# A planner's due times shifted by a table: attention and two expert layers on one core

## The chip, the cores and the metric

The kernel runs on one core of a Trainium2 chip. The metric is the device time of one execution in microseconds, as the median of several runs. A profiled execution has a time of its own and a span, which runs from its first instruction to its last.

## What is computed

Three steps follow each other on 2304 tokens (4 batches of 576). Everything comes in and goes out in float32.

1. Attention with 8 heads of width 64. Heads 0 to 3 see a causal window of 32 keys; heads 4 to 7 see the causal keys whose position agrees with the query's modulo 32. Softmax, then the product with v.
2. `h = x @ w_in` (512 to 2048), then the rational function `g = P(h) / (Q(h) + 1e-6)` with `P = a0 + a1 h + a2 h² + a3 h³` and `Q = 1 + |b0||h| + |b1|h²`, then `g @ w_out` (2048 to 512).
3. `h = x @ w_in` (512 to 1024), softmax of h times h, a layer norm over the 1024 columns, then `@ w_out` (1024 to 512).

## The kernel before

**Number format.** The large products run in float16 with a high and a low part, three matmuls for one. A weight matrix comes in as 64-bit words. `w_load` brings one group of it with one DMA, `w_conv` puts each word's bits together with three VectorE instructions (one `tensor_scalar`, two `scalar_tensor_tensor`) and sums the squares on ScalarE, `w_scales` takes a power of two from that, and `w_split` writes the high part on ScalarE and the low part on VectorE. `w_in` and `w_out` of the first layer have eight groups each ("wi" 0 to 7 and "wo" 0 to 7). All eight wi groups are wanted by the first complete pass of `mm_h`, all eight wo groups by the first `mm_y`.

**Work.** A batch of attention is 12 units: `attn_scores2` or `attn_scores1` (TensorE), `attn_softmax` (row maxima, VectorE), `attn_exp` (ScalarE), `attn_norm` (POOL), `attn_tp`, `attn_tpe`, `attn_pv` (TensorE, ScalarE, TensorE), and `attn_xhi`, `attn_xlo`, which write the block of tokens `xs`. The first layer has nine blocks of 256 tokens with eight groups each. One group is `mm_h` (24 matmuls), about ten elementwise instructions on ScalarE, VectorE and POOL (`a_abs`, `v_q1`, `p_qm`, `v_p2`, `v_p3`, `a_ln`, `a_ex`, `v_t`, `v_rn`, `v_g`, `a_hi`, `p_lo`), and five groups later `mm_y` (24 matmuls). `g_scale` works out the coefficients `ih` and `ac` that `a_abs` needs: 17 tiny POOL instructions and a few of VectorE, once for each batch; it needs the largest |v| of the batch (`v_max`, two long VectorE reductions) and of the weights (`w_pmax`). The second layer takes tiles of 128 tokens (`mm_in2`, the `m_` functions, two transposing DMAs, `mm_out2`, `out_evac`).

**Order.** Nothing is issued while these functions run. `Order.record` collects every call as an operation, numbered in the order of the source: 7549 in all. `Order.run` works out which operation must wait for which (`pre`, `then`), then a due time for each (`first_due`), and four times in turn plans the whole kernel forward (`forward`) and, from the end found, sets new due times (`backward`). The plan that ends first in the planner's own reckoning is kept and `emit` issues its instructions in that order; line 413 is the call that issues them all, which is why every row of the profile bears L413. `forward` goes by time: on each engine it takes, of the operations that could begin within 0.05 us of the earliest, the one with the smallest `due`. Costs of operations, lags between engines, DMA landings, the port that VectorE and POOL share and a rule for TensorE's clock are built into `cost`, `lag` and `forward`. Each engine then carries out its own list strictly in that order, each instruction waiting for what it depends on; the DMAs stand in one list, SP's.

**Which operation has which number** (for the entries of the table that the prediction speaks of): 4 and 5 load q and k of heads 0 and 1, 7 loads the window heads' values `vl`, 11 is wi 0, 14 loads `vs`, 15 is wi 1, 18 and 19 load further q and k, 21 and 27 to 31 are wi 2 to 7, and 32 to 48 build masks and the identity. 49 to 57 are `v_max(0)` and `x_scale(0)`. 58 to 458 are the 12 units of batch 0 with the four pairs of wi groups between them. 459 to 481 are `w_pmax` and the first `g_scale`. 482 to 485 load wo 0 to 3, 486 to 493 load q, k and v of batch 1, and 499 to 556 convert wo 0 to 3 around `mm_h(0, 0)`. 567 to 586 are `g_scale(2)`, for batch 1: 17 POOL instructions and three of VectorE. 637 to 651 and 713 to 732 convert wo 4 to 7. From 733 on the steps of the main loop follow each other, up to 7548.

Of the kernel before, what the change touches and what calls it, by code (L numbers as in the profile page):

```python
# [111 lines left out]
class Order:  # L112
# [136 lines left out]
    def run(self):  # L249
        ops = self.ops  # L250
        for i, op in enumerate(ops):
            op.then = list(op.post)
            for v in op.values:
                v.__dict__.setdefault("users", []).append(i)
        for q in self.queues.values():
            for v, w in zip(q, q[len(q[0].homes):]):
                for j in v.users:
                    if j < w.users[0]:
                        ops[j].then.append(w.users[0])
        for op in ops:  # L260
            op.before = []
        for i, op in enumerate(ops):
            for j in op.then:
                ops[j].before.append(i)
        self.first_due()
        best = None
        for k in range(self.TURNS):
            seq, end, homes = self.forward()
            if best is None or end < best[0]:
                best = (end, seq, homes)  # L270
            if k < self.TURNS - 1:
                self.backward(end)
        _, seq, homes = best
        for v, h in homes:
            v.home = h
        return seq

    TURNS = 4
    WINDOW, ENOUGH = 3.4133, 2800.0
# [1137 lines left out]
```

## Time and profile before

| | us |
|---|---|
| median of 3 runs | 756.23 (755.44 to 756.89) |
| the profiled execution's own time | 757.08 |
| its span | 755.3 |
| TensorE matmul busy | 699.9 (93% of the span) |
| VectorE busy | 547.1 (72%) |
| ScalarE busy | 489.8 (65%) |
| POOL busy | 353.0 (47%) |

The mean granted TensorE clock of the span is 0.948 of 2.4 GHz. In the page's forty slices of the span TensorE is busy for nine tenths or more in every one from the eighth to the thirty-ninth, and of the first seven only in the second; the granted clock is 0.5 to 0.7 in the second to sixth slice and at 0.9 or more in all others.

A row of windows gives, for one stretch, its length, then busy time and count of instructions for PE (TensorE matmul), PEld (its weight loads), DVE (VectorE), ACT (ScalarE) and POOL, then the granted TensorE clock as a share of 2.4 GHz, the mean busy share of the 16 DMA engines and GB/s. A row of the timeline gives start, length, engine, line, operation, what it writes <- what it reads, shapes, count, and in brackets the idle time before it with what ended it. A row of waits gives who waited, for whom, the total, how often, and the longest. In grouped rows the numbers behind the bar are busy us and mean ns of one.

### The profile page before, as it was taken

What the parts mean: (1) busy time and instruction counts of PE and PEld (TensorE: products, weight loads), DVE (VectorE), ACT (ScalarE), POOL (GpSimd) and SP (SyncE); (2) the same over time, 40 slices, a digit from 0 to 9 for tenths busy, and PEclk for the clock granted to TensorE, in tenths of its full rate; (3) what the DMA queues carried; (4) which work ended last, traced back from release to release, by engine and by line L of the source; (5) the groups of instructions that cost most, each with busy time, mean ns of one, the idle gap of its engine ahead of it and who ended that gap; (6) DMA issues with size and microseconds to landing.
All of it is one profiled execution on the core that took longest, in us unless ns stands there. A gap on an engine that the chain in (4) does not pass through costs nothing.

```text
span 755.3 us, 14378 instructions
## 1 busy us (share of the span) xinstructions
PE 699.9 (93%) x5406; PEld 531.7 (70%) x5406; DVE 547.1 (72%) x1114; ACT 489.8 (65%) x1155; POOL 353.0 (47%) x380
## 2 busy tenths in 40 slices
PE   3975368999999999999999999999999999999997
PEld 3763256898888888787777777777776776765443
DVE  6789899689968997787775577576565766644571
ACT  2787558869789679977766676465655646533451
POOL 3233659755689667776434343533534334320000
PEclk9575569999999999999999999999999999999999
DMA  9996801133421321303202010110201011011244
GB/s 270 312 273 167 223 1 34 35 131 127 132 65 60 117 72 34 83 16 62 62 15 43 1 43 1 44 33 10 43 1 43 21 23 43 1 43 43 56 78 103
DMA packets 68101, 55.98 MB, mean 74 GB/s; under 512 B 39616, under 2 KB 56000, under 8 KB 67520
## 3 DMA queue, kind: packets, MB, share of 16 engines
q1 hardware_dynamic: 68032, 55.07, 28.1%
q8 instruction: 42, 0.69, 0.4%
q14 instruction: 27, 0.22, 0.1%
HBM read 40.90 MB, written 4.72 MB: 60 GB/s over the span
## 4 chain that ended last, share of the span: by engine, by line
PE 84%; DVE 7%; ACT 3%; POOL 2%; issue 2%; DMA 1%; SPq 0%; ACTq 0%; DVEq 0%
PE bank L413 46%; PE banks L413 38%; POOL tiny L413 2%; DMA qkb<-in_qk_dram 1%; DVE tiny L413 1%; DVE wi_l L413 1%; DVE T L413 1%; DVE gtb L413 1%; DVE wo_l L413 1%; ACT e L413 1%; DVE p L413 1%; ACT p L413 1%; ACT wo_h L413 0%; DVE bank L413 0%; ACT ysb L413 0%
## 5 line engine op out<-in xcount | busy, mean ns | idle before, releaser
L413 PE MATMUL bank<-xs,wi_h 128*128 128x256 f16 x1152 | 200.0, 278 | 4.0 <-DVE xs L413 2.5
L413 PE MATMUL bank<-xs,wi_l 128*128 128x256 f16 x576 | 159.9, 278 | 1.3 <-DVE wi_l L413 1.3
L413 PE MATMUL banks<-gtb,wo_h 128*128 128x256 f16 x896 | 151.4, 273 | 0.9 <-ACT ysb L413 0.9
L413 PEld LDWEIGHTS <-wi_h 128*128 128x128 f16 x1248 | 124.2, 100 | 30.7 <-issue 4.1
L413 PEld LDWEIGHTS <-wo_h 128*128 128x128 f16 x1152 | 111.7, 98 | 22.1 <-issue 0.9
L413 POOL TENSOR_SCALAR q<-A,aba 128x512 f32<-128x512 f32 x72 | 66.2, 919 | 129.4 <-ACT A L413 129.2
L413 PE MATMUL banks<-gtb,wo_l 128*128 128x256 f16 x448 | 122.1, 273 | 1.7 <-ACT ysb L413 1.7
L413 DVE SCALAR_TENSOR_TENSOR p<-p,ac,bank 128x512 f32<-128x512 f32 x144 | 106.5, 744 | 3.1 <-ACT A L413 0.7
L413 POOL TENSOR_TENSOR gtb<-p,gtb 128x512 f16<-128x512 f32 x56 | 66.8, 1194 | 75.2 <-ACT gtb L413 75.2
L413 DVE TENSOR_TENSOR p<-p,bank 128x512 f32<-128x512 f32 x72 | 49.2, 684 | 69.2 <-ACT p L413 68.7
L413 POOL TENSOR_TENSOR q<-q,A 128x512 f32<-128x512 f32 x72 | 91.7, 1273 | 4.3
L413 PE MATMUL banks<-wi_h,ysb 128*128 128x512 f16 x288 | 90.7, 379 | 0.0
L413 ACT ACTIVATE A<-bank,ih 128x512 f32<-128x512 f32 x72 | 49.6, 689 | 50.8 <-PE bank L413 48.0
L413 DVE SCALAR_TENSOR_TENSOR q<-q,bank 128x512 f32<-128x512 f32 x72 | 49.3, 685 | 34.7 <-ACT bank L413 25.3
L413 PEld LDWEIGHTS <-ysb 128*128 128x128 f16 x432 | 42.1, 98 | 43.8
L413 PE MATMUL bank<-wo_h,T 128*128 128x512 f16 x224 | 70.6, 379 | 0.0
L413 PEld LDWEIGHTS <-wi_l 128*128 128x128 f16 x576 | 57.3, 99 | 12.3 <-issue 3.1
L413 ACT ACTIVATE gtb<-p 128x512 f16<-128x512 f32 x56 | 35.3, 630 | 41.0 <-DVE p L413 41.0
L413 PEld LDWEIGHTS <-wo_l 128*128 128x128 f16 x576 | 56.4, 98 | 7.6 <-issue 0.8
L413 ACT ACTIVATE L<-q 128x512 f32<-128x512 f32 x72 | 45.3, 630 | 24.3 <-POOL q L413 24.0
L413 ACT ACTIVATE p<-bank,ac 128x512 f32<-128x512 f32 x72 | 56.0, 777 | 3.0 <-PE bank L413 3.0
L413 PEld LDWEIGHTS <-T 128*128 128x128 f16 x336 | 32.9, 98 | 34.6
(257 smaller groups left out, 1429.0 us busy)
## 6 DMA issues: line engine op xcount, KB each, us to landing
qkb<-in_qk_dram SPq DMA_DIRECT2D x28, 304.0 KB, 4.6
out_dram<-ot SPq DMA_DIRECT2D x18, 256.0 KB, 2.4
wo_h<-in_w_out_dram SPq DMA_DIRECT2D x4, 1024.0 KB, 5.4
wo_l<-in_w_out_dram SPq DMA_DIRECT2D x4, 1024.0 KB, 7.8
vl<-in_v_dram SPq DMA_DIRECT2D x4, 768.0 KB, 5.1
wi_h<-in_w_in_dram SPq DMA_DIRECT2D x3, 1024.0 KB, 5.4
wi_l<-in_w_in_dram SPq DMA_DIRECT2D x3, 1024.0 KB, 4.9
wo_h<-in_w_in_dram SPq DMA_DIRECT2D x3, 1024.0 KB, 17.3
```

What stands on the lines that cost most here:

```text
L413: getattr(self.real[op.eng], op.call)(*[real(x) for x in op.a], **{k: real(x) for k, x in op.k.items()})
```

## The change

After the four turns the due times of the best turn are put back, each entry of a table `MOVES` is added to them, and the kernel is planned forward once more with the result. An entry is (seed, first, last, by): with seed 0 every operation from `first` up to but not including `last` gets `by` added; with another seed each of them gets `by` times its own number from a normal distribution drawn with that seed. There are 143 entries, 90 with seed 0 and 53 with another, and 61 of them begin below number 1500. No operation is added or left out and none gets other operands, but a buffer's place within its ring follows the order in which the plan asks for it.

```diff
+            due = [op.due for op in ops]
             seq, end, homes = self.forward()
             if best is None or end < best[0]:
-                best = (end, seq, homes)
+                best = (end, seq, homes, due)
             if k < self.TURNS - 1:
                 self.backward(end)
-        _, seq, homes = best
+        _, seq, homes, due = best
+        if self.MOVES:
+            for i, op in enumerate(ops):
+                op.due = due[i]
+            self.moved(self.MOVES)
+            seq, _, homes = self.forward()
...
+    MOVES = (
+        (927833, 2501, 2901, 0.2), (0, 3124, 3128, 2), (335053, 301, 361, 0.2), (764359, 2520, 2580, 2),
+        (473896, 27, 1527, 0.2), (93203, 88, 148, 1), (0, 485, 505, -4), (0, 7015, 7035, 8), (0, 1298, 1299, 2),
...
+        (396215, 2733, 3133, 0.2), (0, 687, 737, 2), (748384, 344, 404, 2), (499587, 290, 490, 1),
+        (0, 1094, 1114, -4), (102561, 888, 948, 0.5), (0, 0, 20, -2), (0, 3024, 3032, 4), (0, 3445, 3495, -2),
...
+        (312986, 1655, 2055, 0.2), (0, 7406, 7426, -1), (0, 567, 587, -8), (0, 1413, 1433, 0.5), (0, 3268, 3269, 2),
...
+        (697731, 419, 619, 0.2), (0, 3752, 3760, 8), (0, 7428, 7478, 4), (64926, 1221, 1281, 1), (0, 4266, 4274, 4),
...
+        (0, 1096, 1100, 4), (584500, 924, 984, 0.2), (0, 3087, 3091, 2), (0, 1, 9, -2), (875455, 312, 372, 0.2),
...
+        (0, 3153, 3173, -0.5), (0, 3030, 3038, 2), (832548, 4037, 4837, 2), (0, 2126, 2134, -8),
...
+        (940811, 1843, 1903, 0.2), (329605, 2882, 3282, 0.2), (0, 6, 56, -1), (0, 3154, 3204, 0.5),
...
+        (777444, 4158, 4558, 0.5), (920252, 280, 340, 0.2), (0, 2945, 2953, -1), (0, 1, 51, 8), (0, 4067, 4071, 2),
...
+    )
+
+    def moved(self, moves):
+
+        import numpy as np
+
+        for seed, first, last, by in moves:
+            x = np.random.RandomState(seed).standard_normal(len(self.ops)) if seed else np.ones(len(self.ops))
+            for i, op in enumerate(self.ops):
+                if first <= i < last:
+                    op.due += by * x[i]
```

## Rows read from the trace of the kernel before

**Rows 1.** Windows, the run in two: up to 131 us, and TensorE's last matmul.

```profile
0.00:131.00 131.00, 82.84 (x523) 66.16 (x523) 113.82 (x228) 85.14 (x241) 64.72 (x84) 0.70 0.68 184
131.00:751.40 620.40, 617.11 (x4883) 465.50 (x4883) 433.26 (x887) 403.99 (x915) 288.26 (x297) 1.00 0.20 51
```

**Rows 2.** Waits of TensorE after 131 us, the longest total.

```profile
PE banks L413 <- ACT ysb L413: 2.6, 5, 0.6
```

**Rows 3.** Windows, the first 131 us in parts, and the tail.

```profile
0.00:12.00 12.00, 1.79 (x8) 1.43 (x9) 6.86 (x13) 1.97 (x2) 5.53 (x23) 1.00 0.88 258
12.00:45.00 33.00, 28.78 (x165) 25.54 (x164) 24.69 (x56) 22.66 (x90) 8.41 (x6) 0.64 1.05 302
45.00:60.00 15.00, 10.52 (x80) 7.53 (x79) 14.23 (x36) 14.53 (x50) 6.29 (x5) 0.78 1.08 271
60.00:80.00 20.00, 11.16 (x54) 6.97 (x54) 20.00 (x33) 11.82 (x25) 9.84 (x5) 0.50 0.60 166
80.00:93.00 13.00, 1.22 (x5) 1.12 (x6) 10.32 (x23) 8.32 (x11) 7.83 (x16) 0.50 0.97 234
93.00:116.00 23.00, 16.20 (x100) 12.59 (x99) 22.93 (x35) 12.76 (x28) 12.76 (x13) 0.67 0.00 1
...
751.40:755.30 3.90, 0.00 (x0) 0.00 (x0) 0.00 (x0) 0.69 (x1) 0.00 (x0) 1.00 0.18 67
```

**Rows 4.** Waits of VectorE between 12 and 131 us, the three longest totals.

```profile
DVE tiny L413 <- PE banks L413: 3.9, 7, 1.7
DVE tiny L413 <- PE bank L413: 2.2, 3, 1.5
DVE tiny L413 <- ACT p L413: 2.1, 2, 1.8
```

**Rows 5.** Timeline of SP's queue, the first three loads.

```profile
0.72 0.39 SPq L413 DMA_DIRECT2D vl<-in_v_dram  x1
1.18 0.42 SPq L413 DMA_DIRECT2D vs<-in_v_dram  x1
1.64 1.19 SPq L413 DMA_DIRECT2D qkb<-in_qk_dram  x2
```

**Rows 6.** The chain that ended last, its first long piece: start, us, what.

```profile
2.25 8.54 DMA qkb<-in_qk_dram
```

**Rows 7.** Timeline of TensorE: two score products of one shape, and two waits.

```profile
16.22 0.41 PE L413 MATMUL bank<-qkb 128*96 128x127 f32 x2
...
19.49 0.37 PE L413 MATMUL banks<-mask_b,ident_b 96*96 96x127 bf16 x2 [2.25 <-ACT p L413]
...
23.07 0.68 PE L413 MATMUL banks<-qkb 128*96 128x127 f32 x2
...
92.37 0.79 PE L413 MATMUL bank<-e,ones_f 128*128 128x128 f32 x2 [8.71 <-DVE e L413]
```

**Rows 8.** Timeline of POOL: tiny instructions of both `g_scale`, and a wait.

```profile
71.24 9.05 POOL L413 TENSOR_SCALAR tiny<-tiny,aba 128x1 f32<-128x1 f32 x3
...
100.57 4.83 POOL L413 TENSOR_SCALAR q<-A,aba 128x512 f32<-128x512 f32 x1 [12.28 <-ACT A L413]
...
109.56 0.65 POOL L413 TENSOR_SCALAR tiny<-tiny,aba 128x1 f32<-128x1 f32 x2
```

**Rows 9.** Timeline of VectorE, first and last of ten instructions from 71.27 us.

```profile
71.27 1.21 DVE L413 SCALAR_TENSOR_TENSOR T<-wo_h,T 128x1024 int32<-128x1024 int32 x1
...
79.03 1.21 DVE L413 SCALAR_TENSOR_TENSOR gtb<-ws,gtb 128x1024 int32<-128x1024 int32 x1
```

**Rows 10.** VectorE's groups by shape up to 131 us, four of them.

```profile
L413 DVE TENSOR_SCALAR scl_wo<-pat_wo 128x2 int32<-128x2 int32 x4 | 2.5, 621 | 0.0
...
L413 DVE SCALAR_TENSOR_TENSOR wi_l<-T,scl_wi,wi_h 128x1024 f16<-128x1024 f32 x1 | 1.9, 1928 | 0.0
...
L413 DVE RECIPROCAL tiny<-tiny 96x4 f32<-96x4 f32 x9 | 1.5, 166 | 0.0
...
L413 DVE SCALAR_TENSOR_TENSOR wi_l<-ysb,scl_wi,wi_h 128x1024 f16<-128x1024 f32 x1 | 1.3, 1272 | 0.0
```

22 rows, old and new, of the table MOVES are left out of this document.

## The prediction, made before the changed kernel was run

> **What bounds the kernel now.** I read the windows first, because a new order can only win where an engine that matters stands still. The run falls in two at 131 us [rows 1]. Behind it TensorE is busy for 617.11 of 620.40 us at a granted clock of 1.00, that is 2.4 GHz, and its longest total wait there is 2.6 us in five pieces [rows 1, 2]. The reader is to see that this part is as long as its matmuls: their number doesn't change, so only 3.3 us are to be had in it. The tail of 3.90 us is one evacuation on ScalarE and the last output's transfer [rows 3].
>
> What is left is the first 131 us. There TensorE is busy for 82.84 us [rows 1], part of it at half the clock. Busy time times the share of clock that is missing, window by window, gives 28.78 x 0.36 + 10.52 x 0.22 + 11.16 x 0.50 + 1.22 x 0.50 + 16.20 x 0.33 = 24.2 us [rows 3] that the full clock would not have needed. So 48.2 us idle and 24.2 us of slow clock lie in the front, about 72 us, against 3 behind it. The engine that paces this front is VectorE: 113.82 of 131 us [rows 1], and from 45 us on nearly without a pause (14.23 of 15, 20.00 of 20, 22.93 of 23) except between 80 and 93 us [rows 3]. It converts the weight groups, and `mm_y` can't start before the last of wo. The DMA engines bear on it up to 60 us, with shares of 1.05 and 1.08 [rows 3].
>
> **How the end follows from the front.** If all that VectorE does in the front is needed before TensorE can run through, the end moves by as much as VectorE's front gets shorter. VectorE has 131 - 113.82 = 17.2 us idle [rows 1], 5.1 of it before 12 us, where nothing has landed yet, and so 12.0 between 12 and 131 us; 8.3 of that lies between 12 and 45 us and 2.7 between 80 and 93 us [rows 3].
>
> **The change part by part.** Nothing is added or removed: the same instructions and DMAs stand in other places of their queues. The sum of each edit is thus what it takes from or adds to the idle time of the front. The table's entries are shifts of due times against other ready work; a shift common to all competitors does nothing.
>
> *First loads.* SP issues `vl`, `vs`, then the first q and k [rows 5], and the chain waits 8.54 us for the latter [rows 6]. The entries that cover them add up to +3 for `vl`, +4 for the first q and k, +5 for `vs` and wi 0. So `vs` (640 KB by its shape, 128 x 1280 words) may fall behind q and k. At 258 GB/s [rows 3] that is 2.5 us. Bounds: 2.5 us won if the swap comes, 1 us lost if `vs` then holds up `v_max` and through it the first `attn_xhi`. The shift is only one unit, so I take 1 us won.
>
> *Batch 0 with the wi groups, operations 58 to 458.* Random shifts of about 0.2 to 2 on every kind of operation. VectorE's waits here are on TensorE (3.9 + 2.2 us) and on ScalarE's exponentials (2.1 us) [rows 4], twelve pieces, each of which another ready conversion could fill. Bounds: 0, because the loads keep the DMA engines full and a conversion can't start before its group has landed, and 8.3. Between them I take 3.5: the waits name engines, not DMAs [rows 4], but a new order fills some holes and opens others.
>
> *First coefficients and wo groups, operations 459 to 732.* The entry of -4 pulls the loads of batch 1 and the first wo conversion ahead, that of +2 pushes wo 6 and 7 back, that of -8 pulls `g_scale(2)` ahead. VectorE's idle here is 12.0 - 8.3 = 3.7 us. Besides, POOL holds it up: `scl_wo` takes 621 ns where a small instruction takes 166, four times, and one `wi_l` takes 1928 where its like takes 1272 [rows 10], together 4 x 0.455 + 0.66 = 2.5 us. Bounds: 0 and 6.2 won; I take 1.5, near the lower end, since the windows there are full already.
>
> *The chain of `g_scale(0)` on POOL.* Three tiny instructions take 9.05 us, where two of the same kind take 0.65 later [rows 8]; 9.05 - 3 x 0.33 = 8.1 us too much, while VectorE runs ten instructions on end, most with two inputs from SBUF, from 71.27 to beyond 79.03 us [rows 9]. TensorE then waits 8.71 us [rows 7]. The planner lets the two engines take turns at the port; the two queues don't keep that. VectorE's work goes on meanwhile, so little of it counts: if the stall went, 8.71 us of TensorE would be freed while VectorE still paces. Bounds: 8.1 won, 8.1 lost if it comes twice. I take 1 us won, near nothing, because no entry addresses it.
>
> The Trainium skill's page "SBUF — State Buffer", section "SBUF: two separate sides", says that whichever of the two engines starts first gets the shared port pair for the whole instruction, while the other "fully blocks". By that a tiny POOL instruction would wait for one VectorE instruction at most, and three for 3 x 1.21 = 3.6 us as an estimate. The trace has 8.1 us [rows 8], so here POOL was passed over more than once; the measurement decides, and by the page the case "slower" below would come out at 756.3 us.
>
> *Behind 131 us.* 82 entries begin at 1500 or later, one spreading operations 4037 to 4836 by 2 times a random number. Covered by TensorE's own queue of ready matmuls: VectorE is busy for 433.26 of 620.40 us [rows 1]. If that cover went, a missing `p` or `xs` would leave TensorE waiting. Bounds: 3.3 us won, and as loss the same 3 us by the nearest row, the waits that are there now [rows 2]. I take 0. The entries at the end (7406 to 7477) meet a TensorE without gaps; 0.
>
> **Sum.** 1 + 3.5 + 1.5 + 1 + 0 = 7.0 us. The profiled execution took 757.08 us, its span of 755.3 and 1.78 around it; less 7.0 that is 750.1. The median of the runs shown, 756.23, stands 0.85 lower, so the same gain gives 749.2 us.
>
> **The rivals.** *A bigger gain through the clock.* Two score products of one shape take 0.41 us at 16.22 and 0.68 at 23.07; between them TensorE waited 2.25 us and its clock fell from 2.4 to 1.2 GHz [rows 7]. If the new order closes that wait, the products of batch 0 could keep 2.4 GHz between 12 and 45 us and give back up to 10.4 us (28.78 x 0.36). For it: VectorE's waits there are mostly on TensorE [rows 4]. Against it: TensorE is busy for 28.78 of those 33 us at a mean clock of 0.64 already [rows 3], so there is not much waiting left to close. The page "TensorE: Matmul & The Clock Gate" of the Trainium skill, "Part 1: The HAM clock gate", puts the clock down to how busy the engine has recently been, and by it this gain would come. With the sum's 7.0 and, say, 8 of the 10.4 it would be 15 us won: 741 us.
>
> *No change.* The loads pace the front to 60 us (shares 1.05 and 1.08 [rows 3]) and VectorE's conversions the rest, so a new order moves holes about and closes none: 756 us. Against it: rows 4 name no DMA.
>
> *Slower: `g_scale(2)` falls among the conversions.* Pulled ahead by 8, its 17 POOL instructions can come to stand where VectorE runs two-input instructions on end. POOL's queue is strict, and behind them stand `v_q1` and `p_qm` of the first groups; ScalarE's `a_ln`, VectorE's `v_t` and with them TensorE's next `mm_h` wait for those. Price: once more 8.1 us [rows 8], less the 3.5 won before it, so 4.6 us: 761 us. It decides from the point where these instructions start before POOL's present pause of 12.28 us ends at 100.57 us, yet outlast it [rows 8]; if they fit inside the pause they cost nothing. For it: `q` took 4.83 us at 100.57 [rows 8]. Against it: they need batch 1's largest |v|, which may not be there so early.
>
> **How the numbers follow.** About 0.2%, or 1.5 us, is what a measurement of this kernel can tell from no change. Forecast (1.5 to 12 us won): 0.58. Clock case (12 to 20 us won): 0.14. No change: 0.08. Slower: 0.20. So faster 0.72, same 0.08, slower 0.20. The range runs from 739 to 760 us: all of the forecast's and of the unchanged case, most of the clock case and the half of the slower case that loses less than 4 us. The bounds added up reach from 756.2 - 2.5 - 8.3 - 6.2 - 3.3 = 736 to 756.2 + 1 + 8.1 + 2.6 = 768 us; their ends need every term to fall one way. The forecast's own range is 744 to 755.
>
> **What would show it.** TensorE should run through from about 125 us instead of 131, and the windows behind that should stay above 99%. VectorE's idle between 12 us and that point should fall from 12.0 to about 7 us, with fewer waits on TensorE and ScalarE. The first q and k should land up to 2.5 us sooner. If the three tiny POOL instructions again take some 9 us, that term is void; if `g_scale(2)`'s do, the slower case is at work. I am wrong in kind if the front is as long as before and the gain or loss lies behind 131 us, or if the front gets shorter with VectorE's idle unchanged, which would mean that TensorE's clock or the loads paced it.

## The result: slower, and the profile after

The changed kernel takes 762.85 us (median of 17 runs), the kernel before 756.89 in the same comparison. The ratio is 1.0066, with a 95% interval of 1.0048 to 1.0083, so about 5 us are lost where 7 were forecast to be won. The profiled execution took 761.67 us, its span 759.9. The 17 executions took 758.81 to 766.38 us, at mean granted clocks between 0.939 and 0.957 of 2.4 GHz, so a trace stands for one of them.

The first part of the page gives each engine's busy time and how many instructions it stands for, of the kernel before and of the changed one:

```profile
PE 699.9 (93%) x5406; PEld 531.7 (70%) x5406; DVE 547.1 (72%) x1114; ACT 489.8 (65%) x1155; POOL 353.0 (47%) x380
```

```profile
PE 708.2 (93%) x5406; PEld 534.9 (70%) x5406; DVE 550.0 (72%) x1114; ACT 489.3 (64%) x1155; POOL 348.8 (46%) x380
```

As many records of matmuls as before, 5406, are busy for 708.2 us instead of 699.9. The windows of the changed kernel, cut at 131 us as in [rows 1], say where:

```profile
0.00:131.00 131.00, 85.58 (x545) 68.43 (x547) 117.90 (x227) 87.53 (x245) 62.85 (x80) 0.73 0.67 184
131.00:756.00 625.00, 622.41 (x4865) 466.47 (x4863) 432.06 (x888) 401.11 (x910) 285.98 (x300) 1.00 0.21 51
```

Up to 131 us there are 22 records of matmuls more. The part behind it should then be shorter: it has 18 fewer (a matmul that lies across the border counts on both sides), at the full clock. Yet it takes 625.0 us instead of 620.4, with 5.3 us more of busy time, and its last matmul ends 0.23 us later still. The busy share stays above 99%, as I had named for a sign, and the waits of TensorE behind 131 us have even become less than in [rows 2]:

```profile
PE banks L464 <- ACT ysb L464: 1.7, 3, 0.6
PE bank L464 <- DVE xs L464: 0.5, 1, 0.5
PE bank L464 <- DVE p L464: 0.2, 1, 0.2
```

So TensorE doesn't wait there; its matmuls have become longer on average. Which ones is seen in its timeline. Each product of `p` and `v` (`attn_pv`) leaves two records, so x8 is four products in a row, all that most units have; a product fills 64 of the 128 columns of TensorE's array only, those of one of the two heads. The changed kernel has whole units and units in pieces:

```profile
143.46 0.38 PE L464 MATMUL banks<-wi_h,wo_h 128*128 128x256 f16 x2
143.77 0.56 PE L464 MATMUL bank<-pts,vl 127*64 127x96 f32 x8
144.26 0.28 PE L464 MATMUL banks<-wi_h,wo_l 128*128 128x256 f16 x1
...
146.55 0.38 PE L464 MATMUL bank<-xs,wi_h 128*128 128x256 f16 x2
146.77 0.27 PE L464 MATMUL bank<-xs,wi_l 128*128 128x256 f16 x1
146.97 0.54 PE L464 MATMUL bank<-pts,vl 127*64 127x96 f32 x6
147.45 0.39 PE L464 MATMUL bank<-xs,wi_h 128*128 128x256 f16 x2
...
149.26 0.27 PE L464 MATMUL banks<-wi_l,wo_l 128*128 128x256 f16 x1
149.47 0.38 PE L464 MATMUL bank<-pts,vl 127*64 127x96 f32 x2
149.78 0.48 PE L464 MATMUL bank<-qkb 128*126 128x126 f32 x2
```

Read the starts, not the lengths, since matmuls overlap. In a run of `mm_h` or `mm_y` each matmul starts 0.11 us after the one before it (two from 146.55 to 146.77). The first product of a piece starts 0.20 us after it (146.77 to 146.97), so every piece costs 0.09 us to enter. From its start to the next matmul, four products take 0.49 us (143.77 to 144.26), three take 0.48 (146.97 to 147.45), and one alone takes 0.31 (149.47 to 149.78). A whole unit thus takes 0.09 + 0.49 = 0.58 us. The same unit parted in three and one takes 0.09 + 0.48 + 0.09 + 0.31 = 0.97 us, 0.39 more. In TensorE's list of instructions the changed kernel has 70 such pieces, the kernel before 50; 48 would be the least, one for each unit. Behind 140 us it is 52 against 34, and 18 more at 0.39 us are 7.0 us. This is an estimate, since six of the twenty parted units are not parted in three and one.

The weight loads of the same moment fit this price:

```profile
146.66 0.10 PEld L464 LDWEIGHTS <-wi_l 128*128 128x128 f16 x1
146.97 0.36 PEld L464 LDWEIGHTS bank<-pts,vl 127*64 127x64 f32 x6 [0.21 <-issue]
147.44 0.11 PEld L464 LDWEIGHTS <-wi_h 128*128 128x128 f16 x2
```

The load for the matmul of 146.77 starts at 146.66, beside the matmul before it. The load for the first product starts only with the product, after the load queue stood still for 0.21 us, and the first load behind the piece (147.44) isn't ahead of its matmul (147.45) either. The Trainium skill's page "TensorE: Matmul & The Clock Gate", Part 3, section "The mechanism", says that a weight load is pulled ahead of running matmuls when it goes to other row groups or to a background buffer, and its list behind that says "only when row_grp differs". These rows show full-height loads drawn ahead of full-height matmuls, so the list's rule doesn't hold here; at the border of a piece nothing is drawn ahead.

The front, finally. VectorE's waits between 12 and 131 us, against [rows 4]:

```profile
DVE tiny L464 <- PE bank L464: 2.7, 3, 1.4
DVE tiny L464 <- ACT p L464: 1.6, 2, 1.4
DVE tiny L464 <- PE banks L464: 1.4, 2, 1.2
```

These three fell from 8.2 to 5.7 us. VectorE is busy for 117.90 us up to 131 us and for 6.86 up to 12 us, so its idle time between is 119 - 111.04 = 8.0 us, where it was 12.0. Some of what it gained went into longer instructions (groups by shape up to 131 us, of before and after, busy us and mean ns behind the bar):

```profile
L413 DVE SCALAR_TENSOR_TENSOR wo_l<-T,scl_wo,wo_h 128x1024 f16<-128x1024 f32 x4 | 5.0, 1272 | 0.0
```

```profile
L464 DVE SCALAR_TENSOR_TENSOR wo_l<-T,scl_wo,wo_h 128x1024 f16<-128x1024 f32 x4 | 6.9, 1752 | 0.0
L464 DVE TENSOR_SCALAR scl_wo<-pat_wo 128x2 int32<-128x2 int32 x4 | 3.4, 850 | 0.0
L464 DVE SCALAR_TENSOR_TENSOR wi_l<-T,scl_wi,wi_h 128x1024 f16<-128x1024 f32 x1 | 1.3, 1273 | 0.0
```

Against [rows 10], `wo_l` takes 1.9 us more and `scl_wo` 0.9 more, and one `wi_l` 0.6 less: 2.2 us of the 4 are gone again.

### The profile page after: what moved, and what is told of

The parts are those of the page before. It is cut to its first block, busy times and chain, and to the rows that moved or that the text cites. A ratio compares the mean times of both kernels' runs of the same rounds, so it can differ in the third digit from the quotient of the medians.

```text
span 759.9 us, 14372 instructions
## 1 busy us (share of the span) xinstructions
PE 708.2 (93%) x5406; PEld 534.9 (70%) x5406; DVE 550.0 (72%) x1114; ACT 489.3 (64%) x1155; POOL 348.8 (46%) x380
## 4 chain that ended last, share of the span: by engine, by line
PE 80%; DVE 9%; ACT 5%; issue 2%; POOL 2%; DMA 1%; SPq 0%; ACTq 0%; DVEq 0%
PE bank L464 44%; PE banks L464 36%; DVE tiny L464 2%; POOL tiny L464 1%; DVE p L464 1%; DVE T L464 1%; DMA qkb<-in_qk_dram 1%; ACT p L464 1%; ACT e L464 1%; DVE wo_l L464 1%; ACT wi_h L464 1%; DVE wi_l L464 1%; DVE gtb L464 1%; DVE q L464 0%; ACT A L464 0%
## 5 line engine op out<-in xcount | busy, mean ns | idle before, releaser
L464 PE MATMUL bank<-xs,wi_h 128*128 128x256 f16 x1152 | 210.3, 278 | 2.0 <-DVE p L464 1.4
L464 PE MATMUL banks<-gtb,wo_h 128*128 128x256 f16 x896 | 157.2, 273 | 1.1 <-ACT ysb L464 1.1
L464 POOL TENSOR_SCALAR q<-A,aba 128x512 f32<-128x512 f32 x72 | 58.8, 817 | 141.8 <-ACT A L464 140.8
L464 PE MATMUL banks<-gtb,wo_l 128*128 128x256 f16 x448 | 119.2, 273 | 0.6 <-ACT ysb L464 0.6
L464 PE MATMUL banks<-wi_h,ysb 128*128 128x512 f16 x288 | 92.7, 379 | 0.0
L464 ACT ACTIVATE e<-bank,tiny 96x127 f32<-96x127 f32 (+2 forms) x132 | 46.1, 357 | 18.0 <-DVE tiny L464 17.5
```

What stands on the lines that cost most here:

```text
L464: getattr(self.real[op.eng], op.call)(*[real(x) for x in op.a], **{k: real(x) for k, x in op.k.items()})
```

## The experiments

Two numbers come from each trace beside its time. **Pieces** is the count of runs of `attn_pv` products in TensorE's list. **Loss** is the time up to TensorE's last matmul less work: every matmul of the list is given the distance between starts that its kind commonly shows behind 140 us (109 ns for `mm_h` and `mm_y`, 216 in the second layer, 107 for a product of `p` and `v`), which makes 656.6 us for all of them; the loss up to 140 us is 140 less the work started by then, the loss behind it is the rest. "At pieces" is the part of the loss behind 140 us that lies at and within `attn_pv` pieces; from the kernel before to the changed one it rises by 7.7 us, where the estimate by starts was 7.0. Ratios are to the kernel before on the same chip.

| kernel | pieces | loss to 140 | loss behind | at pieces | ratio (95%) |
|---|---|---|---|---|---|
| before | 50 | 82.4 | 12.1 | 7.1 | 1 |
| after | 70 | 80.2 | 19.3 | 14.8 | 1.0066 (1.0048 to 1.0083) |
| e1_together | 48 | 77.1 | 10.6 | 6.2 | 0.9945 (0.9921 to 0.9970) |
| e2_pv_apart | 84 | 85.0 | 29.7 | 25.2 | 1.0239 (1.0205 to 1.0272) |
| e3_tp_apart | 50 | 81.0 | 11.9 | 7.1 | 0.9991 (0.9971 to 1.0010) |
| e4_front_only | 56 | 81.1 | 13.7 | 8.8 | 1.0003 (0.9979 to 1.0027) |
| e5_halves_in_turn | 48 | 77.5 | 10.5 | 6.0 | 0.9936 (0.9911 to 0.9962) |
| e6_both_halves_apart | 78 | 81.9 | 18.2 | 13.4 | 1.0072 (1.0046 to 1.0097) |
| e7_front_together | 48 | 77.5 | 11.1 | 6.2 | 0.9943 (0.9921 to 0.9965) |
| e8_back_together | 48 | 81.4 | 10.7 | 6.2 | 0.9974 (0.9952 to 0.9996) |
| e9_whole_in_batch_0 | 68 | 77.5 | 19.3 | 14.8 | 1.0032 (1.0011 to 1.0053) |
| e10_whole_behind_batch_0 | 50 | 80.2 | 10.5 | 6.1 | 0.9943 (0.9918 to 0.9968) |
| e11_before_whole | 48 | 81.8 | 11.1 | 6.2 | 0.9975 (0.9957 to 0.9994) |

My theory: parted `attn_pv` units cost TensorE the time behind 131 us. Rivals: the other cut-up runs of matmuls (transposes, `mm_h`, `mm_y`) cost it; or the changed order of the other engines does.

**The changed kernel with its units whole.** The plan is kept, but each unit's products are issued where the first of them stands.

```diff
-        return seq
+        return self.together(seq)
...
+    def together(self, seq):
+        groups, done, out = {}, set(), []
+        for t, i in seq:
+            if self.is_pv(i):
+                groups.setdefault(id(self.ops[i].a[0].value), []).append(i)
+        for t, i in seq:
+            if i in done:
+                continue
+            for j in groups[id(self.ops[i].a[0].value)] if self.is_pv(i) else (i,):
...
+                out.append((t, j))
+                done.add(j)
+        return out
```

> The changed kernel's order, but the p x v products of a unit (four matmuls, two in the small units) are issued as one piece where the first of them stood. Theory A (broken pieces): behind 140 us the changed kernel has 52 such pieces against 34 before, and entering and leaving them costs TensorE 14.8 us against 7.1; whole again they cost 7.1, so the time falls by about 7.6 us to some 755 us, 0.2% under the kernel before, while VectorE's front stays as in the changed kernel. Theory B (any finer mixing of matmul streams costs; mm_h stands in 198 pieces against 85): nearly nothing comes back, 762 us. Theory C (it is the front's clock and waits that lost): also about 762 us.

Measured: 751.91 us, ratio 0.9945. The windows of this kernel, front and (not to its very end) what follows:

```profile
0.00:131.00 131.00, 84.46 (x576) 67.47 (x577) 120.14 (x236) 89.50 (x253) 64.45 (x83) 0.77 0.67 184
131.00:744.00 613.00, 610.48 (x4832) 459.81 (x4830) 428.12 (x878) 399.00 (x901) 285.43 (x298) 1.00 0.21 52
```

This edit alone turns a loss of 5 us into a gain of 4. The loss behind 140 us falls by 8.7 us, 8.6 of it at pieces, and the loss up to 140 us falls by 3.1 as well, which the price of pieces alone doesn't explain. The lists of all other engines are those of the changed kernel, and `mm_h` still stands in 197 runs (198 in the changed kernel, 85 before). So neither the order of the other engines nor the finer cut of those matmuls cost the time behind 140 us.

**Units parted in the kernel before, and transposes as a control.** A second helper leaves the first half of each group in place and issues the second half behind the next matmul of another kind; the edit concerns `attn_pv` in one kernel and `attn_tp` in the other, from batch 1 on.

```diff
-        return seq
+        return self.apart(seq, self.is_pv, 590)
...
+            late, nxt = g[len(g) // 2:], pe[p + len(g)]
...
+            moved = [x for x in seq[:nxt + 1] if x[1] in late]
+            seq = [x for x in seq[:nxt + 1] if x[1] not in late] + moved + seq[nxt + 1:]
```

> The order of before, but from batch 1 on the p x v products of a unit are parted in the middle: the next matmul of TensorE's list is put between the halves, in 34 of 36 units (pieces 50 to 84). Theory A: a whole group of four cost 0.19 us beside its matmuls, pieces of two 0.25, pieces of one 0.32, so 28 x 0.31 + 6 x 0.37 = about 11 us more than before, 768 us. Theory B: the same number of breaks, but of any kind would do, so the next run would cost the same. Theory C: no change, 757 us.

> Control: the order of before, but from batch 1 on it is the transposes of p that are parted in the middle by the next matmul of TensorE's list, in 36 of 36 units (pieces 48 to 84); the p x v products stay whole. Theory A: no change within 1 us, 757 us, since in both traces a transpose after a matmul of another kind starts 109 ns behind it, as any matmul would. Theory B: as much as the run before, some 768 us. Theory C: 757 us.

Measured: 775.78 us, ratio 1.0239, with 34 units parted, and 756.44, ratio 0.9991, with 36 groups of transposes parted. So cutting a run of transposes costs nothing; cutting `attn_pv` does, and more than 0.39 us for each unit: the time is 8 us above what the first theory had expected. The timeline of the kernel with parted units shows why:

```profile
149.11 0.38 PE L442 MATMUL bank<-xs,wi_h 128*128 128x256 f16 x2
149.42 0.54 PE L442 MATMUL bank<-pts,vl 127*64 127x96 f32 x4
149.89 0.28 PE L442 MATMUL bank<-xs,wi_l 128*128 128x256 f16 x1
150.11 0.54 PE L442 MATMUL bank<-pts,vl 127*64 127x96 f32 x4
150.58 0.39 PE L442 MATMUL bank<-xs,wi_h 128*128 128x256 f16 x2
```

Two products here take 0.47 us (149.42 to 149.89), almost as long as four in a whole unit. These two are of one head, writing the same 64 columns. In a whole unit the second head's products cost only 0.02 us beyond that: the two heads run side by side. A unit parted by heads therefore takes 2 x (0.09 + 0.47) = 1.12 us instead of 0.58, and 34 x 0.54 = 18.4 us, close to the 18.1 of the ratio (0.0239 x 757) and the 18.1 of the column "at pieces" (25.2 - 7.1). The 34 aren't all alike, so part of this closeness is luck: by the same reading of starts, the six units of two products cost 0.43 us more, and units with larger blocks up to 0.69.

**One head after the other, or in turn.** If that reading is right, parts that hold one product of each head should cost less, and the order within a whole unit should not matter.

```diff
+            g[:] = [x for pair in zip(g[:n], g[n:]) for x in pair]
```

> The changed kernel with whole p x v pieces as in the first experiment, but inside a piece the two heads (output partitions 0 to 63 and 64 to 127) come in turn instead of one after the other. Theory A2 (products of the two heads run side by side as long as they stand in one piece; a piece of four takes 490 ns from its first start to the next matmul, a pair of one head alone 476 ns, so the second head costs next to nothing): a piece is already as short as its longer half, so the time stays at 752 us within 2. Theory A (only the number of pieces counts): 752 us as well. If being in turn let the halves overlap better, up to 0.1 us on 36 pieces: 748 us.

> The order of before with the p x v groups of four parted from batch 1 on, 28 of them, as in the second experiment, but each part holds one product of each head. Theory A2: a part with both heads takes what a small unit's pair takes, 93 ns at its entry and 339 to the next matmul, so a group costs 2 x 0.43 instead of 0.09 + 0.49: 0.28 us more, 28 times, 8 us: 765 us. Theory A (a part is a part): what the second experiment had for its 28 groups, about 16 us: 773 us.

Measured: units whole with the heads in turn 751.76 us (0.9936), the same as whole units in the old order. With 28 units of the kernel before parted into one product of each head 762.83 (1.0072), 5.5 us lost, less than either theory had expected and far nearer to A2. Its timeline:

```profile
145.19 0.38 PE L450 MATMUL bank<-xs,wi_h 128*128 128x256 f16 x2
145.51 0.39 PE L450 MATMUL bank<-pts,vl 127*64 127x96 f32 x4
145.82 0.28 PE L450 MATMUL bank<-xs,wi_l 128*128 128x256 f16 x1
```

Two products of different heads take 0.31 us (145.51 to 145.82), as long as one alone. A unit so parted takes 2 x (0.09 + 0.31) = 0.80 us, 0.22 more than whole; 28 x 0.22 = 6.2, where "at pieces" rose by 6.3. The price of a parted unit is thus set by how it is parted: 0.22, 0.39 or 0.54 us.

**The table's halves.** Only entries that begin below 1500, or only the others.

```diff
         for seed, first, last, by in moves:
+            if first >= 1500:
+                continue
```

> The changed kernel with only the 61 entries of the table that begin below operation 1500. Theory A: the front's gain of 2.2 us stays, 6 more p x v pieces than before cost about 1.5 us: 756 us. Theory C (the front lost the time): as slow as the changed kernel, 762 us.

> Only the entries below 1500, with whole p x v pieces. If the gain of the first experiment over the kernel before (5 us) comes from the front: about 753 us; the front-only kernel had 56 pieces, 8 of them extra, some 2 us. If it comes from the finer order behind: 756 us.

> Only the entries from 1500 on, with whole p x v pieces. TensorE's waits above 0.3 us behind 140 us are 4.1 us in all before and 3.2 in the changed kernel, so with the 2 pieces repaired that before had broken at most 1.5 us can be won: 755.5 us. If the finer order behind is the gain: 752 us. If finer mixing of the streams still costs something: above 757 us.

Measured: the front's entries alone 758.54 us (1.0003) with 56 pieces; with whole units 752.52 (0.9943); the other entries with whole units 755.02 (0.9974). The front's entries with whole units do all that the whole table does with whole units (0.9945). The entries behind 1500 with whole units give what whole units give without any table (0.9975, below): apart from parting units they do nothing that can be measured.

**Do the parted units of batch 0 cost the front its gain?** Two units of batch 0 are parted in the changed kernel, the second and the sixth. One kernel mends only these two, another all but these two.

```diff
-            if self.is_pv(i):
+            if self.is_pv(i) and i < 590:
...
-            for j in groups[id(self.ops[i].a[0].value)] if self.is_pv(i) else (i,):
+            for j in groups[id(self.ops[i].a[0].value)] if self.is_pv(i) and i < 590 else (i,):
```

> The changed kernel with the p times v products of a unit put back side by side in batch 0 alone (instructions below 590): there, two groups are parted, and both stand in the front. If those two parted groups are what kept the front's gain at 2.2 us instead of the 5 us that the kernel with all groups whole shows, the loss up to 140 us falls from 80.2 to about 77.2 us, the stretch from 45 to 60 us gets a granted clock near 0.8 instead of 0.5, and the time is 3 us under the changed kernel's, near 759.5. If the parted groups only cost their own 0.2 to 0.3 us each, the time falls by under 1 us, to about 762.

> The changed kernel with the groups whole everywhere but in batch 0, whose two parted groups stay. If parted groups behind the front cost what the alignment says, the loss behind 140 us falls from 19.2 to about 10.6 us and the time by 8 to 9 us, to about 754; the loss up to 140 us stays near 80.2. If the front's missing gain hung on groups behind batch 0 too, the loss up to 140 us falls as well and the time comes near the 751.9 of the kernel with all groups whole.

Measured: 759.44 us (1.0032) with the two mended, 753.39 (0.9943) with all others mended. Against the changed kernel's 1.0066 these are 2.6 and 9.3 us (differences of ratios by 757), as expected of both. Together they would be 11.9 us, yet mending all units brought 9.2 (1.0066 to 0.9945), and with the two still parted the kernel is as fast as with all whole (0.9943 and 0.9945). Each ratio is known to about 0.2%, so the times leave open whether the two units cost 2.6 us or nothing. The loss in the traces moves as the expectations said: up to 140 us from 80.2 to 77.5 in the first and not at all in the second, behind it not at all in the first and from 19.3 to 10.5 in the second. In these traces the front's part is more than two pieces take themselves. The windows from 12 to 60 us, of the changed kernel and of the one with the two units mended:

```profile
12.00:45.00 33.00, 25.57 (x177) 22.17 (x175) 28.64 (x63) 26.36 (x98) 11.37 (x8) 0.80 1.05 302
45.00:60.00 15.00, 12.88 (x72) 10.03 (x72) 12.67 (x31) 12.27 (x43) 4.22 (x3) 0.50 1.10 271
```

```profile
12.00:45.00 33.00, 28.14 (x187) 24.81 (x186) 28.73 (x64) 26.08 (x98) 11.75 (x8) 0.74 1.05 303
45.00:60.00 15.00, 9.87 (x73) 7.12 (x71) 14.92 (x35) 15.00 (x47) 4.75 (x4) 0.77 1.12 273
```

Busy time by the missing share of clock is 25.57 x 0.20 + 12.88 x 0.50 = 11.6 us in the first and 28.14 x 0.26 + 9.87 x 0.23 = 9.6 in the second. So 2.0 of the 2.7 us are slow clock. One score mask of the 11th unit shows it, again in the changed kernel and then in the mended one:

```profile
46.55 0.31 PE L464 MATMUL bank<-mask_b,ident_b 108*108 108x108 bf16 x1
```

```profile
44.62 0.23 PE L482 MATMUL bank<-mask_b,ident_b 108*108 108x108 bf16 x1
```

It starts 1.9 us later in the first and runs at 1.2 GHz, where it has 2.4 GHz in the second. Of the kernels with the table's front entries, the four whose batch 0 has whole units (e1_together, e5_halves_in_turn, e7_front_together, e9_whole_in_batch_0) have a loss up to 140 us of 77.1 to 77.5 us and a granted clock of 0.76 to 0.82 between 45 and 60 us. The three with parted ones (after, e4_front_only, e10_whole_behind_batch_0) have 80.2 to 81.1 us and 0.50. But one order doesn't always get one clock. Up to 140 us the kernel before, e8_back_together and e11_before_whole carry out the same instructions in the same order on every engine, and up to 111 us so do e2_pv_apart, e3_tp_apart and e6_both_halves_apart. Between 45 and 60 us these six were granted 0.78, 0.50, 0.74, 0.50, 0.73 and 0.73. The rows of e8_back_together and of e11_before_whole:

```profile
45.00:60.00 15.00, 11.58 (x63) 8.69 (x63) 13.23 (x29) 12.49 (x42) 3.61 (x3) 0.50 1.09 269
```

```profile
45.00:60.00 15.00, 9.87 (x71) 7.09 (x71) 14.26 (x34) 14.54 (x50) 6.00 (x5) 0.74 1.12 275
```

The first three of the six lose 82.4, 81.4 and 81.8 us up to 140 us, so the traces of one order lie within 1.0 us. The 2.7 to 4.0 us between parted and whole units of batch 0 are more than that. That mending the two units shortens the front is shown for these traces alone, one of each kernel; that it does so by changing the clock is not shown.

**Whole units without the table.** The kernel before with the helper of the first experiment and no other edit.

> The kernel before, without the table, with its two parted groups put back side by side. By the cost of a piece (two pieces fewer, 0.3 us each) the time falls by about 0.6 us, under 0.2%. If keeping groups whole brings something else than the pieces themselves (the order of what follows, the clock of the front), it falls by more than 1.5 us, and then the 5 us by which the changed kernel with whole groups beats the kernel before are not the table's.

Measured: 755.49 us, ratio 0.9975 (0.9957 to 0.9994), 1.9 us less. That lies between the two expectations. Behind 140 us the loss falls by 1.0 us, 0.9 of it at pieces. The 0.6 us by which it is smaller up to 140 us isn't the mending's: both kernels keep one order until 235 us, where the first of the two units stands. The ratio of the table with whole units, 0.9945, is 0.0030 lower, 2.3 us. The intervals overlap a little; the losses up to 140 us (81.8 against 77.1) point the same way and are further apart. The best kernels, all with the table's front entries and with whole units at least behind batch 0, stand at 0.9936 to 0.9945; which of them is the fastest can't be told.

## Why the prediction was wrong

**The step that failed is "Behind 131 us"**, with the sentence on which it rests: that this part "is as long as its matmuls: their number doesn't change, so only 3.3 us are to be had in it". The number didn't change, and the lengths did. I had bounded the loss by the waits that TensorE has there [rows 2], at 3 us, and the loss behind 140 us rose by some 7, outside both bounds. Waits were the wrong measure: a parted unit makes none. It shows as busy time, and so the busy share that I had named as a sign stayed right while 7 us were lost. I never asked what the random shifts do to such groups. The planner didn't ask either: its `cost` prices each matmul by itself, so a parted unit is free in its reckoning, and shifts that differ within a unit part it. With its units whole the same table wins 4.2 us (0.9945), inside the forecast's 1.5 to 12: it is this term, put at 0, that turned the result round.

**The front's terms** were right in kind, and too large in what came of them. Instead of 7.0 us the loss up to 140 us fell by 2.2 (82.4 to 80.2). With the two parted units of batch 0 mended it falls by 4.9, so in these traces the order itself gives some 5 us there; by the ratios with whole units (0.9975 and 0.9945) it is 2.3. A sign that I had named for the front came: TensorE is busy without a break from 123 to 131 us, where before it still paused between 128 and 131 (busy for 2.55 of 3).
- *First loads (1 us):* void. SP issues in the same order as in [rows 5], and the chain's transfer is only 0.2 us shorter than in [rows 6]:

```profile
2.24 8.31 DMA qkb<-in_qk_dram
```

- *Batch 0 and coefficients (5.0 us):* VectorE's idle time fell by 4.0 us, near the 5 forecast, but 2.2 of them went into longer instructions of its own. With the two parted units mended the loss up to 140 us is 2.7 us less, 2.0 of it slow clock in the windows up to 60 us, and VectorE is busy for 119.82 us up to 131 us and idle for 6.0 between 12 and 131.
- *The chain of `g_scale(0)` (1 us):* POOL's timeline, in place of [rows 8]:

```profile
67.86 1.74 POOL L464 TENSOR_SCALAR tiny<-vmax,pmax_wi 128x1 f32<-128x1 f32 x1 [5.66 <-DVE pmax_wi L464]
...
71.01 1.57 POOL L464 TENSOR_TENSOR p<-p,tiny 108x216 f32<-108x216 f32 x1
72.57 2.88 POOL L464 TENSOR_SCALAR tiny<-tiny,aba 128x1 f32<-128x1 f32 x1
75.55 1.37 POOL L464 TENSOR_SCALAR tiny<-tiny 128x1 f32<-128x1 f32 x1
77.02 2.23 POOL L464 TENSOR_SCALAR tiny<-tiny,aba 128x1 f32<-128x1 f32 x1
...
98.10 4.01 POOL L464 TENSOR_SCALAR tiny<-tiny,aba 128x1 f32<-128x1 f32 x3
```

Tiny instructions still take 1.4 to 2.9 us, so the stall came again, only in smaller pieces. Worse, the last unit's `attn_norm` now stands in POOL's queue behind the first of them, which waits 5.66 us for VectorE, and TensorE waits for its `p`. The product of `e` and `ones_f` that waited 8.71 us in [rows 7] waits 2.70 now, but a wait of 6.63 us is new, and the one before this product of `ssq_wo` and `ones_f` grew from 2.77 to 5.49:

```profile
72.63 0.60 PE L464 MATMUL bank<-ident,p 108*108 108x108 f32 x2 [6.63 <-POOL p L464]
...
83.68 0.80 PE L464 MATMUL bank<-e,ones_f 128*128 128x128 f32 x2 [2.70 <-DVE e L464]
...
99.03 0.59 PE L464 MATMUL bank<-ssq_wo,ones_f 128*128 128x2 f32 x2 [5.49 <-ACT wo_h L464]
```

*The bounds added up* leave out the 8.1 us that the chain's own bounds allow as won; their lower end should have been 728 us, not 736.

**The rivals.** *The clock:* not in the changed kernel. Worked out as in [rows 3], slow clock costs its front 24.2 us, as before, with the last stretch to 131 us counted in. *No change:* not so in the front, whose loss fell by 2.2 us, more than the traces of one order differ by (1.0). *Slower through `g_scale(2)`:* the sign came true, by another cause. The instructions came early, from 96.51 us on, and their three tiny ones took 4.01 us (98.10). That is 3.0 too much, worked out as in the prediction, against the 8.1 feared. The Trainium skill's rule of the port ("SBUF — State Buffer", "SBUF: two separate sides") comes near these three, with the 3.6 us estimated from it; it did not for `g_scale(0)` of before. The kernel with the front's entries and whole units has this move as well, and is faster than the kernel before. *Wrong in kind:* of the sign that I had named for this, the half "the gain or loss lies behind 131 us" came true; the front was not as long as before.

## What to carry to other kernels

Before giving a reordering of a busy engine no price, look in the timeline at the distance between starts where one kind of instruction gives way to another, and at what runs side by side: a busy share near 100% hides what the order costs. A planner that moves instructions one by one needs a price for such borders, or must move the group as one; here twenty parted groups cost more than the whole table had won. And a gain in a stage where TensorE's clock wavers should be read from several executions and with the rest of the order held fixed, since there the same order was granted half the clock in one execution and three quarters in another.

## What the runs showed of the hardware

- Two products that fill the two halves of the columns run side by side (blocks of 96 queries, at 2.4 GHz): one alone takes 0.31 us from its start to the next matmul, one of each half 0.31, two of one half 0.47, two of each half 0.49.
- Going from a matmul over 128 columns to a product over 64 costs 0.09 us, and the weight load there starts only with the product; matmuls of full width follow each other at 0.11 us with their loads ahead. Parted transposes cost nothing (0.9991).
- The order of the instructions doesn't fix TensorE's clock: six kernels with the same lists up to 111 us were granted between 45 and 60 us 0.50 of it twice and 0.73 to 0.78 four times.
